# Batch 0 of a windowed attention and mixer kernel: a pair's second and third score chunk issued as one block

## The chip, the cores and the metric

One core of one Trainium2 chip. The metric is the device time of one execution in microseconds (us), less is better. Five engines work beside one another, each through a queue of its own: PE (TensorE, matrix products; PEld is its loading of weights), DVE (VectorE), ACT (ScalarE), POOL (GpSimd) and SP, which here issues transfers. Products land in PSUM banks.

## The reference

Windowed attention with eight global keys and a sloped distance bias, four batches of eight heads, 768 positions, 64 wide; then a low-rank mixer over the positions and a feed-forward layer.

```
scores = q @ k.T / sqrt(64) - slope[h] * dist       # kept: rel in 0..95, or key < 8
a      = softmax(scores) ;  x = a @ v               # (4, 8, 768, 64) -> x: (4, 768, 512)
u      = x + (x.T @ U @ V).T                        # U: 768x32, V: 32x768
out    = u + relu(u @ w_ch1) @ w_ch2                # 512 -> 2048 -> 512
```

## The kernel before

The heads go in pairs, sixteen of them; pairs 0 to 3 are batch 0. Of the scores of a pair only the blocks that the window keeps are computed: for each block of 128 keys the queries of the same block (kT, L365) and those of the next (kA, L372; its first eight columns are the global keys). They lie in a row of 1408 columns per head, cut into three chunks of 512, 512 and 384 columns, c = 0, 1, 2. Both heads of a pair are done for each chunk.

In batch 0 (`st_SE`, L378) the bias is put into PSUM by PE itself: for each head one matmul of the slope times identity with the distance table (L357) starts the accumulation, then the scores add to it, eight matmuls in chunks 0 and 1, six in chunk 2 (`scores`, L347). ACT then takes the exponent from PSUM into the tile ep (L384 or L389). The chunks alternate between two places in PSUM: when i + c is even, one tile of two banks (`ps_sc`, a single buffer; one exponent for both heads, L384), and when it is odd, two banks of the tag cps (one exponent for each head, L389). In later batches the bias is added by DVE (L403), and `scores` is called with on_pe False.

The order of work is written out by hand: each engine takes its instructions in the order of the program text. For batch 0 this is the loop at L747, for pair i:

- S(i,0): the scores and exponents of chunk 0 (L748)
- V(i-1,0): the previous pair's first head times v on PE (L428, L432), then on DVE the reciprocal of the sums (L437) and the product with it (L451), then a cast of x on POOL (L454)
- POOL: the cast of v (L142) and a copy vA of it (L303); further loads are put into the queues of SP and POOL
- for i > 0, T(i+1): twelve transposes on PE (L254), a copy qT on ACT (L276), copies kT and the start of kA on DVE (L277, L282)
- S(i,1) (L767)
- in pair 2, M1(0), the first product of the mixer (L471)
- V(i-1,1), the second head, with its reciprocal and product on DVE; in pair 0 T(1) stands here instead
- DVE: the rest of kA for the next pair (L290, `st_KA`), and the global keys' rows of vA (L316, `st_P`), which V(i,0) needs; the casts of q and k two pairs ahead (L123), on DVE in pair 0 and on POOL in pairs 1 and 2; in pairs 1 and 2 POOL issues a load of w1 (L227)
- S(i,2) (L785), then a copy of x on ACT (L787), and in pairs 2 and 3 M2, which makes uT (L488, L493, L499, L501)

After pair 3 come V(3,0), V(3,1), the last parts of the mixer and the first products of the feed-forward layer (L536, L631). From there the other pairs are interleaved with feed-forward work on PE (`fill`, L716). Its second half needs w2, loaded by POOL's queue (L230), with first use at L666.

Of the kernel before, what the change touches and what calls it, by code (L numbers as in the profile page):

```python
# [20 lines left out]
def kernel(  # L21
# [24 lines left out]
    NP = H // 2  # L46
# [33 lines left out]
    def ps_sc():  # L80

        return psum.tile([P, 2, 512], FP32, name="sc", tag="sc", bufs=1)
# [4 lines left out]
    def ps_cps(name):  # L87
        return psum.tile([P, 512], FP32, name=name, tag="cps", bufs=2)
# [8 lines left out]
    def load_qk(i, behind=None):  # L97

        b, h0 = i // NP, 2 * (i % NP)
        got = []  # L100
        for src, nm in ((q, "qst"), (k, "kst")):
            st = stp.tile([P, 2, NSB, D], FP32, name=nm, tag=nm, bufs=2)
            if behind is not None:
                behind.memset(st[0:1, 0, 0, 0:1], 0.0)
            if i < NPE:
                nc.sync.dma_start(
                    st.rearrange("p h n d -> p h (n d)"),
                    src[b, h0:h0 + 2].rearrange("h (p n) d -> p h (n d)", n=NSB),
                )
            else:  # L110
                nc.sync.dma_start(
                    st.rearrange("p h n d -> p (h n) d"),
                    src[b, h0:h0 + 2].rearrange("h (n p) d -> p (h n) d", p=P),
                )
            got.append(st)
        staged[i] = got
# [15 lines left out]
    def load_v(i):  # L132
        b, h0 = i // NP, 2 * (i % NP)
        st = stp.tile([P, 2 * NSB, D], FP32, name="vst", tag="vst", bufs=2)
        nc.sync.dma_start(
            st, v[b, h0:h0 + 2].rearrange("h (n p) d -> p (h n) d", p=P)
        )
        vsts[i] = st

    def cast_v(i):  # L140
        vt = vbuf[i % NVB]
        nc.gpsimd.tensor_copy(  # L142
            vt.rearrange("p n h d -> p h n d")[:, :, :, 0:D],
            vsts.pop(i).rearrange("p (h n) d -> p h n d", h=2),
        )
        vts[i] = vt
# [67 lines left out]
    def load_uv():  # L214
        nc.gpsimd.dma_start(u16[:, :, 0:R], moe_U.rearrange("(c p) r -> p c r", p=P))
        nc.gpsimd.dma_start(v16w[0:R], moe_V)
# [82 lines left out]
    def st_A(i):  # L299
        vt = vts[i]  # L300
        vA = vap.tile([P, NSB - 1, 2, D + 1], FP16, name="vA", tag="vA")
        if i < NPE:
            nc.gpsimd.tensor_copy(vA, vt[:, 0:NSB - 1])  # L303
            vas[i] = vA
            return
        nc.sync.dma_start(vA[NG:P], vt[NG:P, 0:NSB - 1])
        nc.sync.dma_start(
            vA[0:NG].rearrange("p n h d -> p n (h d)"),
            vt[0:NG, 0:1].rearrange("p n h d -> p n (h d)").broadcast_to(
                (NG, NSB - 1, 2 * (D + 1))  # L310
            ),
        )
        vas[i] = vA
# [33 lines left out]
    def scores(i, c, on_pe):  # L347

        kT, kA, qT = kts[i], kas[i], qts[i]
        c0 = 512 * c  # L350
        tot = min(512, W - c0)
        r0 = 256 if c else 0
        both = None if on_pe and (i + c) % 2 else ps_sc()
        scs = [ps_cps("sc") if both is None else both[:, hi] for hi in range(2)]
        if on_pe:
            for hi in range(2):
                nc.tensor.matmul(  # L357
                    scs[hi][:, 0:tot], slI[:, 2 * (i % NP) + hi],
                    rel16.rearrange("p a c -> p (a c)")[:, r0:r0 + tot], start=True, stop=False,
                )  # L360
        for kb in (2 * c, 2 * c + 1):
            o = 256 * kb - c0
            for hi in range(2):
                r = slice(hi * D, (hi + 1) * D)
                nc.tensor.matmul(  # L365
                    scs[hi][:, o:o + P], kT[r, kb * P:(kb + 1) * P], qT[r, kb * P:(kb + 1) * P],
                    start=(o == 0 and not on_pe), stop=(o + P == tot),
                )
            if kb < NSB - 1:
                for hi in range(2):  # L370
                    r = slice(hi * D, (hi + 1) * D)
                    nc.tensor.matmul(  # L372
                        scs[hi][:, o + P:o + 2 * P], kA[r, kb], qT[r, (kb + 1) * P:(kb + 2) * P],
                        start=False, stop=(o + 2 * P == tot),
                    )
        return scs, both, c0, tot

    def st_SE(i, c):  # L378

        if c == 0:  # L380
            eps[i] = scp.tile([P, 2, W], FP16, name="ep", tag="ep")
        scs, both, c0, tot = scores(i, c, True)
        if both is not None:
            nc.scalar.activation(  # L384
                eps[i][:, :, c0:c0 + tot], both[:, :, 0:tot], AF.Exp, scale=qk_scale
            )
            return
        for hi, sc in enumerate(scs):
            nc.scalar.activation(  # L389
                eps[i][:, hi, c0:c0 + tot], sc[:, 0:tot], AF.Exp, scale=qk_scale  # L390
            )
# [7 lines left out]
    def s_dve(i, got):  # L399
        _, both, c0, tot = got  # L400
        if c0 == 0:
            sps[i] = scp.tile([P, 2, W], FP32, name="sp", tag="sp", bufs=1)
        nc.vector.scalar_tensor_tensor(  # L403
            out=sps[i][:, :, c0:c0 + tot], in0=both[:, :, 0:tot],
            scalar=qk_scale / slope[2 * (i % NP)], in1=relfs[c0 // 512],
            op0=ALU.mult, op1=ALU.add,
        )

    def st_S(i, c):
        s_dve(i, scores(i, c, False))  # L410

    def st_E(i, hi):
        if hi == 0:
# [5 lines left out]
    def st_V(i, hi):  # L419
        b, h = i // NP, 2 * (i % NP) + hi  # L420
        ep, vt, vA = eps[i][:, hi], vts[i], vas[i]
        if hi == 0:
            x16s[i] = xp.tile([P, NSB, P], FP16, name="x16", tag="x16", bufs=3)
        obf = ps_cps("ob") if (i, hi) == (NP - 1, 1) else ps_ob()
        ob = obf[:, 0:NSB * (D + 1)].rearrange("p (n d) -> p n d", n=NSB)
        for qi in range(NSB):
            if qi:
                nc.tensor.matmul(  # L428
                    ob[:, qi], ep[:, OF[qi - 1]:OF[qi - 1] + P], vA[:, qi - 1, hi],
                    start=True, stop=False,  # L430
                )
            nc.tensor.matmul(  # L432
                ob[:, qi], ep[:, DG[qi]:DG[qi] + P], vt[:, qi, hi],
                start=(qi == 0), stop=True,
            )
        rcp = vap.tile([P, NSB], FP32, name="rcp", tag="rcp")
        nc.vector.reciprocal(rcp, ob[:, :, D])  # L437
        xo = xs[b][:, :, h * D:(h + 1) * D]
        x16 = x16s[i][:, :, hi * D:(hi + 1) * D]
        rb = rcp.unsqueeze(2).broadcast_to((P, NSB, D))  # L440
        if i == NP - 1:
            if hi == 1:
                nc.vector.tensor_tensor(x16, ob[:, :, 0:D], rb, ALU.mult)
            else:
                for n in range(NSB):
                    nc.scalar.activation(
                        x16[:, n], ob[:, n, 0:D], AF.Copy, scale=rcp[:, n:n + 1]
                    )
            later.append((xo, ob[:, :, 0:D], rb))
            return  # L450
        nc.vector.tensor_tensor(xo, ob[:, :, 0:D], rb, ALU.mult)  # L451
        if i < NP and hi:
            return x16, xo
        nc.gpsimd.tensor_copy(x16, xo)  # L454
# [292 lines left out]
    for i in range(NP):  # L747
        st_SE(i, 0)  # L748
        if i:
            st_V(i - 1, 0)  # L750
        cast_v(i)
        st_A(i)
        if i < 2:
            load_v(i + 2)
        if i == 0:
            load_uv()
        if i == 1:
            load_qk(NP)
        if i == 2:
            load_qk(NP + 1, nc.gpsimd)  # L760
        if i == 3:
            load_v(NP)
        if i == NP - 1:
            st_M1(i - 2)
        if i:
            st_T(i + 1)
        st_SE(i, 1)  # L767
        if i == 2:
            st_M1(i - 2)
        if i:  # L770
            last_x = st_V(i - 1, 1)
        else:
            st_T(i + 1)
        st_KA(i + 1, nc.vector)
        st_P(i)
        if i == 0:
            cast_qk(i + 2, nc.vector)
        elif i < 3:
            cast_qk(i + 2, nc.gpsimd)
        if i == 1:  # L780
            load_w1(0)
        if i == 2:
            load_w1(1)
            st_R()
        st_SE(i, 2)  # L785
        if i:
            nc.scalar.copy(*last_x)  # L787
        if i >= 2:
            st_M2(i - 2)
    st_V(NP - 1, 0)  # L790
    first = scores(NP, 0, False)
    st_M1(NP - 2)
    st_V(NP - 1, 1)
    cast_qk(NP + 1, nc.gpsimd)
# [138 lines left out]
```

## Time and profile before

| what | value |
|---|---|
| runs before, us | 231.74, 235.61, 232.99; median 232.99 |
| profiled execution, us | 231.74, with a span of 230.0 |
| granted clock of TensorE | 1.000 |
| busy in the span, us | PE 220.7, PEld 171.1, DVE 161.5, ACT 125.8, POOL 72.3 |
| batch 0, from its first bias to the first product at L631 | 6.80 to 33.56 us |
| chunk exponents of batch 0 on ACT | 6.1 us at L389 (x12), 5.7 us at L384 (x6) |
| bias matmuls on record | 22 (of 24), mean 360 ns |

The span runs from the first to the last instruction, and all times below are counted from its start. Busy time is what an engine spent in recorded instructions; some matmul records are missing. Matmuls overlap one another, so what one of them adds to a row of them is read from the chain, where each piece shows only its own advance, and not from its duration. Of a timeline's line the first number is the start, the second the length (for several instructions in a group, of the group), then the engine, the line of the program, the operation and its tiles.

### The profile page before, as it was taken

To read this page: it belongs to the slowest core of one execution; us is meant where nothing else is said; L and a number is where in the kernel's file an instruction comes from. 1 tells how busy PE (TensorE), PEld (TensorE's weight loads), DVE (VectorE), ACT (ScalarE), POOL (GpSimd) and SP (SyncE) were. 2 spreads that over 40 slices of the span, in tenths; PEclk is the share of its full clock that TensorE was granted. 3 is DMA by queue.
4 is the path that set the end of the run, shared out by engine and by line. 5 is a ranking of instruction groups with operands and counts; after the bars stand their busy time and mean duration, and the time that the engine had idled before them with its cause. 6 is when DMAs were issued, how large, how long until landed. Compare 5 with 4: busy or idle time off the path is not lost.

```text
span 230.0 us, 5877 instructions
## 1 busy us (share of the span) xinstructions
PE 220.7 (96%) x2418; PEld 171.1 (74%) x2420; DVE 161.5 (70%) x337; ACT 125.8 (55%) x196; POOL 72.3 (31%) x115
## 2 busy tenths in 40 slices
PE   7989899999999999999999999999999999999993
PEld 2456568788745445888888878888988888888882
DVE  3799876749577979597989897989764444444452
ACT  6787747786805253968485847292732433333320
POOL 6499708297553323123313131313111000000000
PEclk9999999999999999999999999999999999999999
DMA  6999996979999879897979994951321202010022
GB/s 185 335 283 281 281 291 90 321 135 180 191 163 206 201 180 228 203 239 175 261 202 219 242 200 102 144 158 25 88 69 36 94 0 94 0 67 27 10 84 93
DMA packets 86563, 36.68 MB, mean 160 GB/s; under 512 B 74152, under 2 KB 83592, under 8 KB 86536
## 3 DMA queue, kind: packets, MB, share of 16 engines
q1 hardware_dynamic: 81480, 32.01, 57.5%
q0 software_dynamic: 5056, 4.29, 12.4%
q8 instruction: 19, 0.31, 0.6%
q14 instruction: 8, 0.07, 0.1%
HBM read 27.46 MB, written 6.29 MB: 147 GB/s over the span
## 4 chain that ended last, share of the span: by engine, by line
PE 67%; DVE 15%; DMA 7%; ACT 4%; POOL 2%; issue 1%; SPq 0%; ACTq 0%
PE hps L631 25%; PE cx L684 13%; PE cy L684 10%; PE cps L666 8%; DMA w<-in_moe_w_ch_dram 6%; DVE sp L403 3%; PE sc L365 2%; ACT ep L415 2%; DVE x_sb L451 2%; PE tp L254 2%; PE ob L432 2%; DMA kst<-in_k_dram 2%; PE sc L517 1%; PE ob L428 1%; DVE s L555 1%
## 5 line engine op out<-in xcount | busy, mean ns | idle before, releaser
L631 PE MATMUL hps<-uT,w 128*128 128x256 f16 x756 | 96.0, 273 | 0.0
L636 ACT ACTIVATE htr<-hps 128x512 f16<-128x512 f32 x96 | 56.4, 598 | 58.0 <-PE hps L631 57.9
L631 PEld LDWEIGHTS <-w 128*128 128x128 f16 x756 | 70.5, 98 | 9.9 <-issue 0.2
L403 DVE SCALAR_TENSOR_TENSOR sp<-sc,relcat 128x1024 f32<-128x1024 f32 (+1 forms) x36 | 40.7, 1131 | 9.1 <-ACT ep L415 4.8
L415 ACT ACTIVATE ep<-sp 128x1408 f16<-128x1408 f32 x24 | 33.1, 1380 | 0.7 <-DVE sp L403 0.6
L684 PEld LDWEIGHTS <-htr 128*128 128x128 f16 x288 | 27.5, 98 | 3.6
L454 POOL CAST x<-x_sb 128x384 f16<-128x384 f32 x27 | 14.5, 538 | 49.8 <-DVE x_sb L451 45.7
L689 DVE TENSOR_TENSOR x_sb<-cx,x_sb 128x256 f32<-128x256 f32 x36 | 15.2, 422 | 18.3 <-PE cx L684 17.7
L666 PE MATMUL cps<-w,htr 128*128 128x512 f16 x96 | 24.0, 379 | 0.4 <-DMA w<-in_moe_w_ch_dram 0.4
L525 POOL CAST x<-x_sb 128x768 f16<-128x768 f32 x12 | 11.0, 916 | 40.8 <-DVE x_sb L522 40.8
L684 PEld LDWEIGHTS <-s 128*128 128x128 f16 x216 | 20.2, 98 | 2.9 <-DVE s L555 0.6
L689 DVE TENSOR_TENSOR x_sb<-cy,x_sb 128x256 f32<-128x256 f32 x27 | 11.4, 423 | 12.5 <-PE cy L684 12.3
L365 PEld LDWEIGHTS <-kT 64*128 64x128 f16 x192 | 8.3, 93 | 13.7 <-issue 12.4
L451 DVE TENSOR_TENSOR x_sb<-ob,rcp 128x384 f32<-128x384 f32 x30 | 16.7, 558 | 1.0
L365 PE MATMUL sc<-qT,kT 64*128 64x128 f16 x192 | 16.8, 221 | 0.3 <-DVE x_sb L522 0.2
L432 PE MATMUL ob<-v,ep 128*128 128x65 f16 x192 | 16.4, 193 | 0.0
L432 PEld LDWEIGHTS <-ep 128*128 128x128 f16 x192 | 13.8, 98 | 3.1 <-ACT x L787 0.7
L428 PE MATMUL ob<-vA,ep 128*128 128x65 f16 x160 | 14.5, 194 | 1.2 <-DVE vA L316 1.2
L142 POOL CAST v<-vst 128x768 f16<-128x768 f32 x16 | 14.0, 877 | 2.9 <-DMA vst<-in_v_dram 2.9
L372 PE MATMUL sc<-qT,kA 64*128 64x128 f16 x160 | 14.3, 217 | 0.6 <-DVE kA L290 0.4
L666 PEld LDWEIGHTS <-htr 128*128 128x128 f16 x96 | 8.4, 97 | 8.5 <-issue 0.5
L522 DVE TENSOR_TENSOR x_sb<-sc,x_sb 128x768 f32<-128x768 f32 x12 | 11.5, 956 | 4.6 <-PE sc L517 4.6
(109 smaller groups left out, 315.0 us busy)
## 6 DMA issues: line engine op xcount, KB each, us to landing
qst<-in_q_dram SPq DMA_DIRECT2D x16, 384.0 KB, 4.7
kst<-in_k_dram SPq DMA_DIRECT2D x16, 384.0 KB, 6.1
vst<-in_v_dram SPq DMA_DIRECT2D x16, 384.0 KB, 4.0
out_dram<-x_sb SPq DMA_DIRECT2D x23, 256.0 KB, 3.1
w<-in_moe_w_ch_dram POOLq DMA_DIRECT2D x8, 512.0 KB, 8.1
vA<-v SPq DMA_DIRECT2D x8, 152.3 KB, 3.0
out_dram<-x_sb SPq DMA_DIRECT2D x2, 128.0 KB
uT<-x SPq DMA_TRANSPOSE x12, 3.1
```

The lines of the kernel that those rows point to most:

```text
L365: nc.tensor.matmul(scs[hi][:, o:o + P], kT[r, kb * P:(kb + 1) * P], qT[r, kb * P:(kb + 1) * P], start=(o == 0 and not on_pe), stop=(o + P ...
L403: nc.vector.scalar_tensor_tensor(out=sps[i][:, :, c0:c0 + tot], in0=both[:, :, 0:tot], scalar=qk_scale / slope[2 * (i % NP)], in1=relfs[c0 ...
L415: nc.scalar.activation(eps[i][:, hi], sps[i][:, hi], AF.Exp, scale=slope[2 * (i % NP)])
L428: nc.tensor.matmul(ob[:, qi], ep[:, OF[qi - 1]:OF[qi - 1] + P], vA[:, qi - 1, hi], start=True, stop=False,)
L432: nc.tensor.matmul(ob[:, qi], ep[:, DG[qi]:DG[qi] + P], vt[:, qi, hi], start=(qi == 0), stop=True,)
L451: nc.vector.tensor_tensor(xo, ob[:, :, 0:D], rb, ALU.mult)
L454: nc.gpsimd.tensor_copy(x16, xo)
L631: nc.tensor.matmul(hps[:, k * FT:(k + 1) * FT], w1_16[:, dc, jt * P:(jt + 1) * P], uT[:, dc, ts], start=(dc == 0 and k == 0), stop=(dc == ...
L636: nc.scalar.activation(cell["htr"][:, 2 * jp:2 * jp + 2].rearrange("p j t -> p (j t)"), hps, AF.Relu)
L666: nc.tensor.matmul(cps, htr[:, jc, t * P:(t + 1) * P], w2_16[:, jc], start=(b > 0 and jc == 0), stop=(jc == NJC - 1),)
L684: nc.tensor.matmul(ps, cell[a][:, j], weight(w, j), start=(first and j == 0), stop=(done is not None and j == HJ - 1), skip_group_check=True,)
L689: nc.vector.tensor_tensor(x_sb[:, n, cs], ps, x_sb[:, n, cs], ALU.add)
```

## The change

In the loop over batch 0, the call for chunk 2 is taken from its place after V(i-1,1) and the DVE copies, and joined to that for chunk 1: `st_SE(i, 1, 2)`. `scores` becomes a generator that stops after the biases. So PE gets, in this order: chunk 1's two biases, chunk 2's two biases, chunk 1's eight score matmuls, chunk 2's six; ACT gets chunk 1's exponents and then chunk 2's. The PSUM tiles of both are taken with the biases. Chunk 0 is a call by itself as before, and the later batches call `scores` through a helper that runs it to its end.

```diff
@@ scores
                     scs[hi][:, 0:tot], slI[:, 2 * (i % NP) + hi],
                     rel16.rearrange("p a c -> p (a c)")[:, r0:r0 + tot], start=True, stop=False,
                 )
+        yield
         for kb in (2 * c, 2 * c + 1):
...
-        return scs, both, c0, tot
-
-    def st_SE(i, c):
-
-        if c == 0:
+        yield scs, both, c0, tot
+
+    def chunk(*args):
+
+        return list(scores(*args))[1]
+
+    def st_SE(i, *cs):
+
+        if 0 in cs:
             eps[i] = scp.tile([P, 2, W], FP16, name="ep", tag="ep")
-        scs, both, c0, tot = scores(i, c, True)
+        made = [scores(i, c, True) for c in cs]
+        for m in made:
+            next(m)
+        for got in [next(m) for m in made]:
+            exps(i, *got)
+
+    def exps(i, scs, both, c0, tot):
         if both is not None:
...
     def st_S(i, c):
-        s_dve(i, scores(i, c, False))
+        s_dve(i, chunk(i, c, False))
@@ the loop over batch 0
-        st_SE(i, 1)
+        st_SE(i, 1, 2)
         if i == 2:
             st_M1(i - 2)
         if i:
...
         if i == 2:
             load_w1(1)
             st_R()
-        st_SE(i, 2)
         if i:
             nc.scalar.copy(*last_x)
...
-    first = scores(NP, 0, False)
+    first = chunk(NP, 0, False)
```

## The prediction

> In what follows S(i,c) are the scores of pair i, chunk c, V(i,h) the product with v of its head h, T(i) its transposes; a pair's three chunks are 0, 1, 2. "vA copy" on DVE is L316, "kA copy" on DVE is L290; POOL has a vA copy of its own (L303).
>
> **What bounds the kernel now.** First the page's slices.
>
> ```profile
> PE   7989899999999999999999999999999999999993
> DVE  3799876749577979597989897989764444444452
> PEclk9999999999999999999999999999999999999999
> ```
>
> PE is full from the seventh slice (about 34 us) on, at full clock; only before that is there room. The waits of PE after 34 us sum to 1.1 us. So batch 0 (6.8 to 33 us) is a lead-in whose length is added to a PE-bound rest. Second, busy time by pair in that lead-in:
>
> ```profile
> 10.58:15.31 4.73, 4.07 (x66) 2.49 (x64) 4.54 (x12) 3.77 (x7) 4.60 (x7) 1.00 1.17 324
> 15.31:20.88 5.57, 5.23 (x77) 3.27 (x76) 4.83 (x11) 4.70 (x8) 5.50 (x10) 1.00 1.24 274
> 20.88:27.50 6.62, 5.45 (x81) 3.49 (x80) 6.52 (x14) 5.01 (x10) 5.11 (x8) 1.00 1.19 275
> ```
>
> The columns are length, PE, PEld, DVE, ACT, POOL. In the stretches of pairs 1 to 3 DVE works 4.54 of 4.73, 4.83 of 5.57 and 6.52 of 6.62 us; POOL is nearly as full; ACT has most room. Third, the chain that ended last:
>
> ```profile
> 9.07 0.99 PE tp L254 x12
> 10.06 0.02 issue
> 10.09 0.96 DVE kT L277
> ...
> 13.64 0.15 issue
> 13.79 0.23 PE sc L365 x2
> 14.02 0.06 PE sc L372 x2
> ...
> 14.67 0.21 DVE rcp L437
> 14.88 0.02 issue
> 14.90 0.56 DVE x_sb L451
> 15.46 0.66 DVE kA L290
> 16.12 0.78 DVE vA L316
> 16.90 0.04 issue
> ```
>
> It runs T(1), DVE's copies, S(1,1), V(0,1), DVE's reciprocal and product, the kA and vA copies, V(1,0), T(3), and so on: no exponent of chunk 1 or 2 is on it, but V(i-1,1), which the change puts behind chunk 2, is. In pair 1 and pair 2 DVE stands waiting for V(i-1,1) (14.55 to 14.67; tmp and rcp behind PE at 19.4 and 19.7); in pair 3 rcp starts at 25.46, right when V(2,1) ends (25.41). Fourth, the two engines whose copies overlap:
>
> ```profile
> 16.04 0.84 DVE L316 COPY vA<-v 8x520 f16<-8x520 f16 x1
> 26.62 0.84 DVE L316 COPY vA<-v 8x520 f16<-8x520 f16 x1
> 15.87 0.87 POOL L123 CAST q<-qst 128x768 f16<-128x768 f32 x1
> 26.45 0.87 POOL L123 CAST q<-qst 128x768 f16<-128x768 f32 x1
> ```
>
> The vA copy ends 0.14 us after a POOL cast in pairs 1 and 3 (16.88 after 16.74, 27.46 after 27.32) and 0.15 in pair 2 (22.26 after 22.11); in pair 0, with no POOL cast beside it, it takes 0.27. The kA copy ends 0.19 to 0.20 after the POOL operation it overlaps in all four pairs (11.74, 16.12, 21.42, 26.70 after 11.55, 15.93, 21.22, 26.50). I read it so: a DVE copy that starts during a POOL copy or cast finishes only 0.14 to 0.20 us after that one ends.
>
> **The change part by part.** No instruction is added or removed, nothing on SP, DVE or POOL changes place in its queue. On PE, chunk 2's biases (two) go ahead of chunk 1's scores, and its six score matmuls ahead of T(1) in pair 0, V(i-1,1) in pairs 1 to 3, and also M1(0) in pair 2. On ACT, chunk 2's exponents pass only pair 0's successor: the qT copy of T(1).
>
> What is moved, on PE: two 512-column biases take 0.43 us in the chain, so two of 384 take 0.32; six scores 3 x 0.06 = 0.17. Together 0.49 us ahead of V(i-1,1). The 0.15 us stop between bias and scores (13.64) was there for chunk 1 already; chunk 2 loses its own, but off the path, since behind it PE waits for DVE anyway (0.2, 0.3 and 0.65 us for the vA copy). Its gain is between 0 and 0.15 a pair; I take 0.
>
> Pair 0, a new wait: chunk 2's biases write the same two-bank tile as chunk 0, which the exponent at L384 reads from 7.93 to 8.95. Before, chunk 1's scores went out at 8.36; now they, chunk 2's scores and T(1) are queued behind the waiting bias (PE keeps order: before 27.52 it idles 0.65 us although later work is ready). 8.97 + 0.32 + 0.15 + 0.41 (chunk 1) + 0.17 (chunk 2) = 10.02; transposes 0.83 (as at 32.89) end at 10.85, where before it was 10.06: +0.79. The kA copy then starts at 11.96, after POOL's vA copy (11.55), and is not held: its length is between 0.26 (a 384-column copy, L267) and 0.57; at 0.4 it gives 0.1 back. The exponents of chunks 1 and 2 (1.0 + 0.81, from 9.87) stand before the qT copy, which ends at 12.47 instead of 10.77; S(1,0), released at 11.79 by the kA copy before, gets going at 12.49 and is 0.76 late. T(2) follows at about +0.75. I take +0.75, between 0.65 and 0.87.
>
> Pair 1: V(0,1), reciprocal and product are late by 0.75 + 0.49, so the kA copy comes at 15.46 + 1.24 = 16.70. POOL's queue moves only by 0.52 (its x cast waited for its own queue until 13.84, now for the product at 14.31 + 0.05). Its vA copy ends at 16.45, so the kA copy misses that gap by 0.25, falls into the q cast, and the vA copy into the k cast, ending 18.09: the vA copy ends at 18.23 for 16.88, +1.35.
>
> Pair 2: POOL follows the product of V(1,0), +1.28. The kA copy comes at 20.50 + 1.35 + 0.49 = 22.34, still inside the q cast (ends 22.50), as before it did. The vA copy ends 0.14 behind the k cast, 23.53 for 22.26: +1.27. Here the 0.49 costs nothing: POOL's casts cover it.
>
> Pair 3: POOL again follows DVE, +1.27. The kA copy comes at 26.23 + 1.27 + 0.49 = 27.99, after POOL's vA copy (27.77), and is held by the q cast, the vA copy by the k cast, to 28.15 + 1.27 + 0.14 = 29.56 for 27.46: +2.10. V(3,0), its scaling on ACT and M1(3) follow.
>
> Without holding, the same rows add up plainly: 0.87 + 3 x 0.49 = 2.34. The range for the lead-in is so 0.5 (both gaps of pairs 1 and 3 met) to 2.5 (pair 2's q cast missed too, +0.4); I take 2.1, because the seven ends are met by the holding.
>
> The Trainium skill, "SBUF — State Buffer", section "Who interferes with whom", says that VectorE and GpSimd share one pair of ports as an exclusive lock, so that of two such operations the one that starts second waits for the whole of the first. By that rule the loss goes in steps of a cast, as above, and not by the plain sum of 2.34; the seven ends agree with it.
>
> Behind the lead-in all is moved alike. PE waits once for the last w2 load (0.39 us before 65.83, landing 13.6 us after issue, with DMA at 1.23 of its share). POOL issues it late too, but if the landing is set by the traffic, up to 0.39 is absorbed; I take 0.2. Sum: 2.1 - 0.2 = +1.9. The profiled execution took 231.74 us (span 230.0 and 1.74 around it), so 233.6 for it; it was the fastest of the three shown, whose median is 232.99: 234.9.
>
> **The rivals.** *The gaps are met.* If V(i-1,1) is late by less than 0.25 us and not 0.49 (biases that overlap better than their 0.16 each), the kA copies of pairs 1 and 3 still start ahead of the q cast. Then pair 1 costs POOL's 0.5, pair 3 nothing: 233.5 to 234.3. Against it: missed by 0.25 and 0.22, by rows of 0.06 and 0.43 that hardly vary.
>
> *Not slower.* Chunk 2's scores and exponents are ready a step earlier; if the next V(i,0) begins without its wait, the 0.22, 0.33 and 0.65 us that PE stood there go, 1.2 in all, against 0.75 in pair 0: -0.45, 232.5. For it: the first weights of V(3,0) waited 0.7 for ACT. Against: the matmul after it waited for DVE's vA copy each time, and that one comes later, not earlier. It decides only if the vA copy ends before the exponents do (16.14 and 26.91), where it now ends at 16.88 and 27.46. The weaker form, that nothing is lost since PE has idle time in 6.8 to 27.5, falls by T(1) and V(i-1,1) being on the chain.
>
> *Worse.* ACT's qT copy in pair 0, 1.7 us late, and pair 2's missed cast add up to 0.4 each, 235.7. For over 2% (237.7) another 2 us would have to come from transfers: the q and k loads of pair 4 leave SP 0.5 us later, behind POOL's release of the v buffer, but are cast 1.3 us later, so they gain slack.
>
> **How the numbers follow.** Forecast (+1.7 to +2.4) 0.5; gaps met (+0.5 to +1.5) 0.2; not slower 0.12; worse 0.18, of it over 2% 0.07. A measurement of this kernel, with runs from 231.74 to 235.61, can tell about 2% from no change. Faster by over 2% would need -4.7 us, over twice all the PE waits that could go: 0.03. Within 2%: 0.9; slower 0.07. Range: 232.4 (not slower) to 237.0 (worse, 235.7, and the scatter of the runs above their median, half of 2.6).
>
> **What would show it.** T(1) starting near 10.0 instead of 9.07; the first score of chunk 1 right after 9.4 and not 8.36; qT of pair 1 ending near 12.5; DVE idle about 0.5 us before the reciprocal of V(0,1); the vA copies of pairs 1 to 3 ending 0.14 us after the k casts, at 18.2, 23.5, 29.6; PE full from about 36. I am wrong if the kA copy of pair 1 or 3 starts before the q cast, if T(1) starts before 9.6, or if PE's waits after 34 us change by more than 0.5.

## The result and the profile after

The changed kernel is slower. Its median is 233.99 us (22 runs, 232.38 to 236.43) against 231.75 us of the kernel before in the same comparison (22 runs): ratio 1.0096, 95% interval 1.0068 to 1.0123, so 2.2 us (1.6 to 2.8). Ratios leave out slow executions, more than 1.5% above the fastest of their kernel, such as one of 440.86 us of the kernel before. A second comparison on another occasion gave 1.0062 (1.0034 to 1.0090), 1.4 us. The profiled execution took 232.53 us with a span of 230.7, only 0.7 us more span than the profile shown of before; it is one of the fastest of its kernel, and that a single pair of profiles misleads here comes up again below.

In the changed file the lines behind L361 lie 1 to 11 further: the scores are L366 and L373, the two forms of the exponent L395 and L400, the reciprocal L448, the product L462, the last users of w2 L677.

The page's slices after:

```profile
PE   7879799999989999999999999999999999999993
DVE  3687867658578979597989897989754344444452
PEclk9999999999999999999999999999999999999999
```

As before, PE is full from about the seventh slice on; only the lead-in differs. Busy time in the stretches from one pair's first bias to the next (length, PE, PEld, DVE, ACT, POOL):

```profile
10.42:15.91 5.49, 3.91 (x64) 2.54 (x63) 4.63 (x12) 4.58 (x8) 4.67 (x6) 1.00 1.22 284
15.91:21.62 5.71, 5.01 (x75) 3.40 (x76) 4.52 (x10) 4.56 (x8) 4.50 (x9) 1.00 0.90 223
21.62:28.25 6.63, 5.42 (x83) 3.61 (x82) 6.06 (x15) 4.97 (x11) 6.04 (x8) 1.00 1.10 252
```

DVE does about the same work (4.63, 4.52, 6.06 for 4.54, 4.83, 6.52 us) but stands longer: its gap in pair 1 grew from 0.19 to 0.86 us, in pair 2 from 0.74 to 1.19 and in pair 3 from 0.10 to 0.57. The chain of waits after:

```profile
8.82 0.48 PE sc L357 x2
...
9.80 0.79 PE tp L254 x12
...
10.64 0.82 ACT ep L395
11.46 0.70 ACT qT L276
...
15.45 0.21 DVE rcp L448
...
16.24 0.74 DVE kA L290
16.98 0.78 DVE vA L316
```

Chunk 2's biases of pair 0 do start only at 8.82, 0.04 us after chunk 0's exponent, with chunk 1's scores behind them; T(1) begins at 9.80 and not 9.07. New on the chain are chunk 0's exponent (from 7.75), which chunk 2's biases wait for, and the exponent of chunk 2 with the qT copy behind it. In pair 1 DVE waits 0.59 us for V(0,1). The vA copies on DVE, and POOL's k casts beside them:

```profile
16.90 0.84 DVE L316 COPY vA<-v 8x520 f16<-8x520 f16 x1
21.89 0.85 DVE L316 COPY vA<-v 8x520 f16<-8x520 f16 x1
27.89 0.27 DVE L316 COPY vA<-v 8x520 f16<-8x520 f16 x1
```

```profile
16.73 0.87 POOL L123 CAST k<-kst 128x768 f16<-128x768 f32 x1
22.61 1.28 POOL L123 CAST k<-kst 128x768 f16<-128x768 f32 x1
27.92 0.92 POOL L123 CAST k<-kst 128x768 f16<-128x768 f32 x1 [0.15 <-DMA kst<-in_k_dram]
```

In pair 1 the vA copy ends 0.14 us behind the k cast, at 17.74 (16.90 + 0.84). In pair 2 it ends 0.14 behind the q cast (22.60), which had waited for its load until 21.67; in pair 3 it slips in before the k cast and takes 0.27. So the vA copies are 0.86, 0.48 and 0.70 us later than in the profile of before, not 1.35, 1.27 and 2.10.

### The profile page after: what moved, and what is told of

The parts are those of the page before. It is cut to its first block, busy times and chain, and to the rows that moved or that the text cites. A ratio compares the mean times of both kernels' runs of the same rounds, so it can differ in the third digit from the quotient of the medians.

```text
span 230.7 us, 5878 instructions
## 1 busy us (share of the span) xinstructions
PE 219.6 (95%) x2417; PEld 171.2 (74%) x2420; DVE 160.7 (70%) x337; ACT 125.6 (54%) x196; POOL 72.4 (31%) x115
## 3 DMA queue, kind: packets, MB, share of 16 engines
HBM read 27.46 MB, written 6.29 MB: 146 GB/s over the span
## 4 chain that ended last, share of the span: by engine, by line
PE 70%; DVE 12%; DMA 8%; ACT 5%; POOL 2%; issue 1%; SPq 0%; ACTq 0%
PE hps L642 25%; PE cx L695 13%; PE cy L695 10%; PE cps L677 8%; DMA w<-in_moe_w_ch_dram 6%; DVE sp L414 3%; PE sc L366 3%; ACT ep L426 2%; DVE x_sb L462 2%; PE tp L254 2%; PE ob L443 2%; DMA kst<-in_k_dram 2%; PE ob L439 2%; PE sc L528 1%; PE sc L373 1%; DVE s L566 1%
## 5 line engine op out<-in xcount | busy, mean ns | idle before, releaser
L700 DVE TENSOR_TENSOR x_sb<-cx,x_sb 128x256 f32<-128x256 f32 x36 | 15.2, 422 | 18.3 <-PE cx L695 17.7
L677 PE MATMUL cps<-w,htr 128*128 128x512 f16 x96 | 24.0, 380 | 0.7 <-DMA w<-in_moe_w_ch_dram 0.7
L366 PEld LDWEIGHTS <-kT 64*128 64x128 f16 x192 | 8.5, 93 | 13.2 <-issue 11.2
L462 DVE TENSOR_TENSOR x_sb<-ob,rcp 128x384 f32<-128x384 f32 x30 | 16.7, 558 | 1.0
L366 PE MATMUL sc<-qT,kT 64*128 64x128 f16 x192 | 16.1, 221 | 1.2 <-ACT qT L276 1.0
L677 PEld LDWEIGHTS <-htr 128*128 128x128 f16 x96 | 8.4, 97 | 8.8 <-issue 0.8
L373 PE MATMUL sc<-qT,kA 64*128 64x128 f16 x160 | 13.8, 217 | 0.4 <-DVE kA L290 0.4
```

Of the source, the lines that this page charges most:

```text
L366: nc.tensor.matmul(scs[hi][:, o:o + P], kT[r, kb * P:(kb + 1) * P], qT[r, kb * P:(kb + 1) * P], start=(o == 0 and not on_pe), stop=(o + P ...
L373: nc.tensor.matmul(scs[hi][:, o + P:o + 2 * P], kA[r, kb], qT[r, (kb + 1) * P:(kb + 2) * P], start=False, stop=(o + 2 * P == tot),)
L677: nc.tensor.matmul(cps, htr[:, jc, t * P:(t + 1) * P], w2_16[:, jc], start=(b > 0 and jc == 0), stop=(jc == NJC - 1),)
L700: nc.vector.tensor_tensor(x_sb[:, n, cs], ps, x_sb[:, n, cs], ALU.add)
```

## The experiments

The question is which part of the change costs, and by what. *Place*: chunk 2's PE work now stands ahead of T(1) and of V(i-1,1), which DVE waits for. Rivals: *ACT's order* in pair 0 (the qT copy behind two chunks' exponents); *mixing* (the two chunks' biases ahead of both scores); *joining* (the exponents of a pair in one block, wherever it stands). Ratios are to the kernel before in the same comparison.

**1. The changed kernel again** (no edit).

> The changed kernel once more, for a second profile and more times. Its first profile lost only 0.7 us in span while the medians differ by 2.2 us. If the loss goes in steps of POOL's casts (place theory), this second profile may show other steps: the vA copy of pairs 1, 2, 3 ends either 0.14 us after the k cast (late: 18.2, 23.5, 29.6) or after the q cast; and the time should follow the number of late steps. If instead the loss is a plain sum, every profile should show the same shifts. Time +1.7 to +2.6 us either way.

Measured: 1.0062 (1.0034 to 1.0090). The steps are others than in the first profile: the vA copies end at 18.50, 23.74 and 29.13, and the span is 232.2. So the end times vary from one execution to the next; they do in the kernel before too (16.88, 22.26, 27.46 in its first profile, 17.73, 22.45, 27.07 in that of experiment 12).

**2. Joined in pair 0 alone.**

```diff
-        st_SE(i, 1, 2)
+        st_SE(i, 1, 2) if i == 0 else st_SE(i, 1)
...
             st_R()
+        if i:
+            st_SE(i, 2)
```

> Chunks 1 and 2 joined in pair 0 alone, the old order in pairs 1 to 3. Place theory (work put ahead of T(1) and V(i-1,1) is paid where DVE waits for it): about +0.75 us at T(2), +0.5 to +0.9 us in time. Rival (the loss is ACT's order in pair 0, exponents ahead of the qT copy): nearly the whole loss, +1.8 to +2.2.

Measured: 0.9994 (0.9966 to 1.0022), at most half a microsecond lost. ACT's order falls. The 0.75 that place was to cost in pair 0 does not show in the time either, although in this profile T(1) was late (10.15) and T(2) with it (13.29, where the profile of before has 12.45).

**3. Joined in pairs 1 to 3 alone.**

```diff
-        st_SE(i, 1, 2)
+        st_SE(i, 1, 2) if i else st_SE(i, 1)
...
             st_R()
+        if i == 0:
+            st_SE(i, 2)
```

> Chunks joined in pairs 1 to 3, the old order in pair 0. Place theory: V(i-1,1) is 0.49 us late in each pair, pair 2 covered by POOL's cast: +0.8 to +1.6 us in time, and with pair0_only it adds up to the whole. Rival (ACT's order in pair 0): 0 to +0.3.

Measured: 1.0075 (1.0048 to 1.0103), 1.7 us (1.1 to 2.4), just above the 0.8 to 1.6 expected. The loss lies in pairs 1 to 3.

**4. Moved, not mixed.**

```diff
-        st_SE(i, 1, 2)
+        st_SE(i, 1)
+        st_SE(i, 2)
```

> Chunk 2 stands behind chunk 1 as in the changed kernel, but chunk 1 is finished first: biases, scores, exponents of 1, then of 2. Place theory: pair 0 no longer stops chunk 1's scores at chunk 0's bank (T(1) ends about 0.4 later than before, not 0.8), pairs 1 to 3 as in the changed kernel: +1.3 to +1.9 us. Rival (the mixing of the biases is what costs): 0 to +0.5.

Measured: 1.0088 (1.0061 to 1.0115), 2.0 us, where 1.3 to 1.9 were expected. Standing together costs nothing that can be told from this; standing earlier costs. Mixing falls.

**5. The joined block behind V(i-1,1)** in pairs 1 to 3, pair 0 in the old order.

```diff
-        st_SE(i, 1, 2)
+        if i == 0:
+            st_SE(i, 1)
         if i == 2:
             st_M1(i - 2)
         if i:
             last_x = st_V(i - 1, 1)
+            st_SE(i, 1, 2)
...
+        if i == 0:
+            st_SE(i, 2)
```

> In pairs 1 to 3 the joined block stands behind V(i-1,1) (and M1(0)) and not ahead of it; pair 0 has the old order. Same biases together, same exponents together. Place theory (the loss is the work ahead of V(i-1,1), which DVE waits for): nothing of the loss is left, V(i-1,1) comes even 0.4 to 1 us earlier than in the kernel before, where DVE can use 0 to 0.35 of it in pairs 1 and 2: -0.6 to +0.3 us. Rival (joining the chunks costs wherever it stands, by later first exponents): +1 to +2 us.

Measured: 1.0018 (0.9992 to 1.0044). With the same chunks joined, but V(i-1,1) first, the loss is gone (0.4 us, -0.2 to 1.0). Joining falls as a cost of the sum, place stands. Step by step joining is not neutral: counted from T(2), the reciprocal of V(1,0) comes at +5.28, in the order before at +4.92 (experiment 12), because PE's biases for chunk 0 of pair 2 waited 0.95 us for the joined block's exponent; that of V(2,0) comes at +10.07 in place of +10.48. Losses and gains cancel here. In this profile PE's first products at L631 began 1.2 us sooner than in the profile of before, and PE then waited 1.99 us for w2. What followed, in stretches of 2 us (the third number from the end is the granted clock):

```profile
66.00:68.00 2.00, 1.76 (x6) 0.70 (x6) 0.29 (x1) 0.00 (x0) 1.17 (x2) 0.68 0.54 87
68.00:70.00 2.00, 2.00 (x11) 0.59 (x9) 1.00 (x2) 0.00 (x0) 0.00 (x0) 0.50 0.82 172
70.00:72.00 2.00, 2.00 (x20) 0.94 (x15) 1.72 (x3) 0.56 (x2) 0.00 (x0) 0.97 0.50 114
```

The clock fell to a half for some 3.4 us. By these rows that takes 0.64 + 1.0 + 0.06 = 1.7 us of PE's time (an estimate), and the span is 1.6 us longer than the sum that fits the other profiles (below).

**6. and 7. w2 issued earlier**, in the order before and in the changed one.

```diff
-        if i == NP + 1:
-            load_w2(0)
-            load_w2(1)
+        if i in (NP, NP + 1):
+            load_w2(2 * (i - NP))
+            load_w2(2 * (i - NP) + 1)
         if i + 2 < NPE:
             cast_qk(i + 2, nc.gpsimd)
-        if i == NP + 1:
-            load_w2(2)
-            load_w2(3)
```

> The kernel before, with w2's first two blocks issued one pair earlier, so that the last two are issued where the first two were, 3 us earlier. In the profiles so far the span is the start of the first products at L631, plus PE's wait for the last w2 block (0.4 to 1.9 us), plus 195.8 to 196.0. Theory (that wait is in every execution and makes much of the scatter): the wait is gone, -0.4 to -1.5 us, and runs lie closer together. Rival (the wait only takes the place of a later one): 0 +- 0.3.

> The changed kernel with the same earlier w2. Against the kernel before: if the lead-in's lengthening passes whole to the end, the difference to w2_early_before stays at 1.5 to 2.2 us; if part of the loss was a longer wait for w2 (0.7 and 1.2 us in the two profiles, 0.4 before), the difference shrinks to about 0.7 to 1.5 us.

Measured: 0.9965 (0.9931 to 0.9998) and 1.0058 (1.0017 to 1.0098). The wait is gone from both profiles, but the times lie no closer together (229.3 to 234.3 and 230.9 to 235.5). Between the two the changed order still costs about 1.0058 / 0.9965 = 1.0093, 2.1 us. Each was compared with the kernel before and not with the other, so this carries the noise of both, roughly 1 to 3 us; but the loss is there without any wait for w2, and w2 is not its cause.

**8. The vA copy on ACT**, in the order before.

```diff
     def st_P(i):
-        nc.vector.tensor_copy(
+        (nc.vector.tensor_copy if i >= NP else nc.scalar.copy)(
...
-        st_P(i)
...
         st_SE(i, 2)
+        st_P(i)
```

> The kernel before, with the copy of the global keys' rows of vA (L316, pairs 0 to 3) on ACT behind the exponents of chunk 2, and so off DVE. Theory (a DVE copy that starts beside a POOL copy or cast is held to 0.14 us behind its end, and these ends are the steps of the lead-in): V(1,0), V(2,0) start 0.1 to 0.7 us earlier, -0.3 to -0.8 us in time, and no DVE copy waits for the k cast. Rival (the copy is long by itself, 0.8 us for 8x520): ACT takes as long, 0.6 to 0.9, and with ACT held by it the time is the same or longer, 0 to +0.8.

Measured: 1.0006 (0.9979 to 1.0033). The copy takes 0.61 us on ACT, behind chunk 2's exponents. That it no longer waits for POOL brings no time that can be told; the expected gain is not there.

**9. to 11. The same with w2 earlier**: 5 with 6, 8 with 6, and 5, 6 and 8 together.

> joined_late with w2 issued earlier. In joined_late the first products at L631 came 1.2 us sooner than in the kernel before, but PE then waited 2.0 us for w2, and its granted clock was 0.50 for some 3 us after that wait. Theory (a shorter lead-in was there and w2's landing took it back): the wait and the clock's dip are gone, and it is 0.8 to 1.5 us faster than w2_early_before (whose ratio to the kernel before was 0.9965), 229.2 to 230.1 us. Rival (joining the chunks costs elsewhere): as w2_early_before, or up to 1 us slower.

> vA_on_act (the old order) with w2 issued earlier. Its lead-in was 1.6 us shorter, and PE waited 1.8 us for w2. Theory (DVE's held copy is a step of the lead-in, hidden there only by w2): 1 to 1.7 us faster than w2_early_before, 229.0 to 229.9 us. Rival (the copy's hold is not what sets the lead-in): as w2_early_before.

> joined_late, the vA copy on ACT and w2 earlier, together. If both shorten the same chain by different waits, the lead-in is 2 to 2.6 us shorter than before: 228.3 to 229.2 us. If ACT becomes the bound of a pair (its copies then stand behind later exponents), nothing beyond the better of the two.

Measured: 1.0004 (0.9981 to 1.0028), 0.9989 (0.9956 to 1.0022), 1.0061 (1.0037 to 1.0085). The gains that I expected of the first two are not there. I had taken the early lead-ins of 5 and 8 for their own merit, against one profile of before. But v of pair 0 had landed early in both (POOL's first v cast began at 9.52 and 9.37 us, in that profile of before at 9.91), and the rest of that profile's lead-in is the longest of the old order (counted below). In the profile of joined_late_w2 v landed late, and that lead-in ends at 33.54. The times of vA_on_act_w2 reach from 229.5 to 236.3, and why they scatter so is open. In the third kernel ACT has become the bound, as its chain shows:

```profile
16.10 1.02 ACT ep L395
17.12 0.77 ACT ep L400 x2
17.89 0.49 ACT vA L316
...
18.82 0.67 PE tp L254 x12
```

The vA copy stands behind exponents that stand behind V(i-1,1), so V(i,0) and T(i+2) wait for ACT: slower, where I had expected at worst no gain.

**12. The kernel before again** (no edit).

> The kernel before once more, for a second profile: start of the first products at L631 near 33.6 (33.2 to 33.9), PE's wait for w2 between 0.4 and 2 us, and the span their sum plus 195.8. If its lead-in were as late as 34.2 to 35.2, as in the profiles of the changed order, the loss would not lie in the lead-in.

Measured: one run, 231.1 us, span 229.3. It makes a pair with experiment 1 that shows the loss step by step, since v landed alike in both. First the kernel before, DVE's reciprocals of V(0,1), V(1,1) and V(2,1) with the kA copy of pair 1, then POOL's first v cast, then PE's wait for w2:

```profile
15.53 0.20 DVE L437 RECIPROCAL rcp<-ob 128x6 f32<-128x6 f32 x1
...
16.23 0.73 DVE L290 COPY kA<-kT 128x580 f16<-128x580 f16 x1
...
20.56 0.20 DVE L437 RECIPROCAL rcp<-ob 128x6 f32<-128x6 f32 x1
...
25.65 0.19 DVE L437 RECIPROCAL rcp<-ob 128x6 f32<-128x6 f32 x1
```

```profile
10.82 0.83 POOL L142 CAST v<-vst 128x768 f16<-128x768 f32 x1 [3.82 <-DMA vst<-in_v_dram]
```

```profile
65.40 1.02 PE L666 MATMUL cps<-w,htr 128*128 128x512 f16 x4 [0.36 <-DMA w<-in_moe_w_ch_dram]
```

And the changed order:

```profile
16.02 0.20 DVE L448 RECIPROCAL rcp<-ob 128x6 f32<-128x6 f32 x1 [0.61 <-PE ob L443]
...
16.73 1.01 DVE L290 COPY kA<-kT 128x580 f16<-128x580 f16 x1
...
21.70 0.20 DVE L448 RECIPROCAL rcp<-ob 128x6 f32<-128x6 f32 x1
...
27.42 0.20 DVE L448 RECIPROCAL rcp<-ob 128x6 f32<-128x6 f32 x1 [0.40 <-PE ob L443]
```

```profile
10.82 0.83 POOL L142 CAST v<-vst 128x768 f16<-128x768 f32 x1 [3.83 <-DMA vst<-in_v_dram]
```

```profile
68.31 1.02 PE L677 MATMUL cps<-w,htr 128*128 128x512 f16 x4 [1.21 <-DMA w<-in_moe_w_ch_dram]
```

In these two executions pair 0 loses nothing: DVE's kT copy of T(1) begins at 10.61 in both, its vA copy at 12.50, the reciprocal of V(0,0) at 13.64 and 13.65. The reciprocals of V(0,1), V(1,1), V(2,1) are then late by 0.49, 1.14 and 1.77, those of V(1,0), V(2,0), V(3,0) by 0.78, 1.28 and 2.05 (18.22 and 19.00, 23.78 and 25.06, 27.57 and 29.62). The first products at L631 begin at 33.16 and 35.22, +2.06; PE's wait for w2 adds 0.85; the spans differ by 2.9. From V(1,0) to V(1,1) it takes 2.34 and 2.70, from V(2,0) to V(2,1) 1.87 and 2.36. What pairs 1 and 3 lose beyond 0.49 is the kA copy: POOL's vA copy held it before, the q cast behind that holds it after (0.73 and 1.01 us in pair 1, 0.53 and 0.82 in pair 3).

In the profiles without a clock dip the span is the start of those products, plus the wait for w2, plus 195.6 to 196.0 us. The start itself depends on when v of pair 0 lands, so I count from T(2): with the old order in pairs 1 to 3, 19.86 to 21.11 us (four profiles, pair0_only among them, mean 20.3); with chunk 2 ahead of V(i-1,1), 21.23 to 21.91 (five, mean 21.5); with V(i-1,1) first, 20.32 and 20.31 (all_three, where ACT is the bound, has 21.52). The old order and the changed one do not overlap, though narrowly: 21.11 is the profile of before that the prediction was made from.

## Why the prediction came out right, point by point

The difference was forecast as +1.9 us and measured as +2.2 (1.6 to 2.8), and 233.99 lies in the range. The level of 234.9 is 0.9 too high: its base, 232.99, was the median of three runs, where 22 give 231.75. Of the terms of the sum, not all were right.

- *Chunk 2's 0.49 us ahead of V(i-1,1)*: right, and the cause of the loss. The matched pair shows 0.49 at the first place where it acts (15.53 to 16.02), and by experiments 3, 4 and 5 no other part of the change costs in sum.
- *Pair 0, +0.75*: the wait for chunk 0's bank and the late T(1) and qT copy came as forecast (8.82 for 8.97, T(1) at 9.80 in place of about 10.0, qT ending at 12.15 for 12.47), but the step "T(2) follows at about +0.75" holds only where v lands early. With an early v and the changed order in pair 0, T(2) came 6.25 us after the first bias (the first profile after, and pair0_only); with the old order there it came 5.65 and 5.35 after it (the profile of before, joined_late). Where v lands late (POOL's first v cast from 10.40 on, six profiles), DVE's vA copy of pair 0 waits for POOL's, DVE's casts for T(2) stand behind it, and T(2) comes 2.47 to 2.53 us after that v cast begins, in either order. So it is in the matched pair (13.30 and 13.31), where the v cast waited 3.8 us for its load. There the late T(1) did not even reach DVE: the first bias came 0.41 us sooner in the changed kernel, and the cast of pair 1's k waited for its load until 9.44 and 9.45. The profile of before showed the wait for v too (2.90 us), ending just early enough not to matter. Measured alone: -0.1 us (-0.8 to 0.5), which rules out a constant 0.75 and leaves room for a part of it.
- *Pairs 1 to 3, 2.10 - 0.75 = +1.35*: 1.7 (1.1 to 2.4) in experiment 3. By pair the matched profiles give 0.78, 0.50 and 0.77 where the working had 0.60, -0.08 and 0.83. The 0.60 and 0.83 are near, and the missed gap of the kA copy that they rest on is what the matched pair shows. Pair 2 was mis-sized: I let POOL's casts cover its 0.49. In the matched pair they did not, since there the old order's vA copy was not held at all (0.27 us, begun before the k cast).
- *Steps of POOL's casts, and not a plain sum*: the holding is real. Over the fourteen profiles 73 copies at L290 and L316 began with a POOL copy or cast under way: 62 ended 0.14 to 0.20 us after it; ten, begun in its last 0.1 us, took 0.33 us, and one, begun within 0.01 us of POOL's start, 0.27. In batch 0 the vA copy takes 0.27 to 0.29 when it is not held, the kA copy 0.33 to 0.52. That agrees with the lock of the Trainium skill, "SBUF — State Buffer", "Who interferes with whom": of two such operations the second waits for the whole of the first. But the forecast end times (18.2, 23.5, 29.6) were met by neither profile of the changed kernel throughout, because POOL's casts themselves wait for the q and k loads, by up to 0.43 us in them. And with the vA copy taken off DVE the time stayed (1.0006). The matched pair's 2.05 is more than the plain 3 x 0.49 = 1.47, by the kA copies; whether the median loss is too is open: 1.7 (1.1 to 2.4) holds both.
- *w2 absorbs 0.2*: wrong in sign in the profiles. The wait grew from 0.4 (both profiles before) to 0.7 and 1.2; in the matched pair by 0.85, more than the 0.5 by which the prediction said it would be wrong. Landing moves with POOL's issue, which the lead-in moves too. That this growth is regular is not shown: pair0_only had 1.9 us of it in its profile, without a loss in its median.

That the sum came out this near is luck in part: what pair 0 did not cost was made up by pair 2 and, in the profiles, by w2. The rival "the gaps are met" asked for the kA copies of pairs 1 and 3 ahead of the q cast, and in both profiles of the changed kernel they came behind it. In that of w2_early_after they did begin ahead of it, by 0.01 and 0.02 us, which the prediction had named as a sign of being wrong; its 21.23 us from T(2) are still more than the 20.23 of w2_early_before. Something like the rival came through late loads: in the first profile after, pair 2's kA copy began 0.02 us before a q cast that had waited 0.43 us for its load, and pair 3's vA copy 0.03 us before a k cast that had waited 0.15. "Not slower" and "worse" did not come.

The fastest kernel of the study is the order before with w2 issued earlier, 0.9965 (0.9931 to 0.9998), only just clear of no change; nothing built on the joined block beat the kernel before.

## What to carry to other kernels

On an engine that works in order, look not at how much is moved but at what it now stands ahead of: half a microsecond on PE, which has idle time to spare there, costs about its length in every pair, because the fullest engine waits for what was pushed back; put the other way round, the same block costs nothing that can be told. Before a late step is added to a sum, look for another input of the same consumer that waits for a load: if that load arrives later in other executions, the step is hidden there, and one profile may show it just barely in time. Take a second profile of both kernels before single steps are compared.

## What the runs showed of the hardware

A wait of PE of 1.99 us was followed by a granted clock of 0.50 for some 3.4 us (experiment 5), while 1.9 us in experiment 2 was not followed by any dip. The Trainium skill, "TensorE: Matmul & The Clock Gate", Part 1, has the clock fall to half after an idle window of about 3.4 us; the half agrees, the length of the wait was shorter here. The last w2 block took 13.6 to 15.2 us from issue to landing in the nine profiles with the old place of its load, with PE's wait for it from 0.4 to 2.0 us, and v's first cast began anywhere from 8.95 to 10.89 us over all fourteen, with T(2) from 12.05 to 13.36. Single executions differ by such waits almost as much as by the change.
